# Sliding-window attention rewritten around 32-row scores that are made twice

## The chip, the cores and the metric

The kernel runs on one core of one Trainium2 chip. The metric is the device time of one execution in microseconds; the kernel before takes 2570.04 us (median of three runs, 2560.99 to 2573.86). All inputs and outputs are bf16. "Granted clock" is the share of full TensorE speed that the records of the run show. In the lines of the profiles PE is TensorE, PEld its weight loads, DVE VectorE, ACT ScalarE, POOL GpSimd and SP the queue of transfers. Each trace is of one execution.

## The reference, cut to what matters

```python
g = sigmoid((x * gate_w).sum(-1, keepdims=True))
a = A(x, wqkv, wo)         # 32 heads of 20 columns, causal window of 256 of 2048 rows
b = B(x, mem0, Wq, ...)    # 64 segments in sequence, each hands 8 memory rows on
return g * a + (1 - g) * b

# A, the sliding branch
scores = einsum('bhqd,bhkd->bhqk', q, k) * 20 ** -0.5
mask = (i - j >= 0) & (i - j < 256)
p = softmax(where(mask, scores, -1e9)); o = einsum('bhqk,bhkd->bhqd', p, v) @ wo
```

The kernel computes A first, block by block (16 blocks of 128 rows), then the projections of the memory rows that B needs (called the tail here), then B (the recurrent branch), then the mix. Only A is rewritten. Because of the window, a block of 128 queries meets three blocks of keys.

## The kernel before: what the change touches

Per head, the scores of a block are three 128x128 products. They contract all 128 rows: the queries of one head of four are kept in a tile that is zero in the other 96 rows (`QTm`), the keys of four heads lie together. The masks are added by further products.

```python
def st_scores(h):
    g, r = h // 4, h % 4
    sp = ps_s.tile([P, 512], FP32, name="s_ps", tag="s")
    for ci, c in enumerate(kbs):
        need_mask = (c == qb) or (c == qb - (NKB - 1))
        nc.tensor.matmul(sp[:, ci * P:(ci + 1) * P], lhsT=qm[r][:, g, :], rhs=kring[c][:, g, :],
                         start=True, stop=not need_mask)
        if need_mask:
            nc.tensor.matmul(sp[...], lhsT=ident[:], rhs=(m_last if c == qb else m_first)[:], start=False, stop=True)
    nmx = hp.tile([P, 1], FP32, name="a_nmx")
    nc.vector.tensor_reduce(out=nmx[:], in_=sp[:, 0:nk * P], axis=AX.X, op=ALU.max, negate=True)
    nc.scalar.activation(out=ex[:, 0:nk * P], in_=sp[:, 0:nk * P], func=ACT.Exp, bias=nmx[:], scale=1.0)

def st_transpose(h):      # for two heads: 6 transposes into pt_ps, then one copy to SBUF
    ...
    nc.tensor.transpose(pt_ps[:, a, ci, :], ex[:, ci * P:(ci + 1) * P], ident[:])
    ...
def st_pv(h):             # values: transposed probabilities times V, with a column of ones for the sum
    ...
```

The block ends with the output projection. The B weights that stay in SBUF are loaded in two parts: 34 tiles of 384 KB early, during A, and the rest after A.

```python
early, late, last = weights.resident[:34], weights.resident[34:-3], weights.resident[-3:]
...
branch_A(...)                                   # takes the early ones along
for u in late:
    weights.load_resident(post, u, nc.gpsimd)   # all issued at A's end
tail_projections(tc, weights, xTb, xbqk, xbv)
```

## Time and profile before

| Stage (profiled run, us) | before |
|---|---|
| first maximum | 26.4 |
| sliding branch ends (first tail product) | 526.1 |
| tail projections | 180.9 |
| recurrent branch | 1834.1 |
| mix | 30.0 |
| span | 2571.1 |
| granted clock in the branch, 130 us to 60 us before its end | 0.954 |

The stages are cut at the first product of the next stage in the trace. The page's slices, the table by stretch, the chain and the groups that this rests on are in the prediction. One row of the page is not there and will matter: the granted clock, in tenths, in 40 slices of 64.3 us. The kernel before runs at full speed nearly everywhere:

```profile
PEclk9999999899999999999999999999999999999996
```

### The profile page before, as it was taken

What the parts mean: (1) busy time and instruction counts of PE and PEld (TensorE: products, weight loads), DVE (VectorE), ACT (ScalarE), POOL (GpSimd) and SP (SyncE); (2) the same over time, 40 slices, a digit from 0 to 9 for tenths busy, and PEclk for the clock granted to TensorE, in tenths of its full rate; (3) what the DMA queues carried; (4) which work ended last, traced back from release to release, by engine and by line L of the source; (5) the groups of instructions that cost most, each with busy time, mean ns of one, the idle gap of its engine ahead of it and who ended that gap; (6) DMA issues with size and microseconds to landing.
All of it is one profiled execution on the core that took longest, in us unless ns stands there. A gap on an engine that the chain in (4) does not pass through costs nothing.

```text
span 2571.1 us, 114087 instructions
## 1 busy us (share of the span) xinstructions
PE 2226.3 (87%) x49877; PEld 1645.7 (64%) x49893; DVE 1198.7 (47%) x3578; ACT 1124.3 (44%) x2433; POOL 702.2 (27%) x1973
## 2 busy tenths in 40 slices
PE   7889888889889888888888888888888888889885
PEld 5777777679456665666656666656666566566663
DVE  5777777623234443444444344434443344344434
ACT  4777777622234333433333343333333343333333
POOL 7622222040122222222222222222222222222220
PEclk9999999899999999999999999999999999999996
DMA  6600000075578888888888888888888888888887
GB/s 210 202 17 18 17 17 15 9 252 148 144 242 277 265 263 263 276 266 278 269 259 269 271 275 266 264 256 270 265 266 270 255 268 273 268 266 270 268 258 228
DMA packets 293747, 561.63 MB, mean 218 GB/s; under 512 B 104568, under 2 KB 114048, under 8 KB 293248
## 3 DMA queue, kind: packets, MB, share of 16 engines
q1 hardware_dynamic: 266032, 495.28, 60.5%
q0 software_dynamic: 24256, 55.62, 7.3%
q8 instruction: 391, 6.41, 1.0%
q10 hardware_dynamic: 2960, 3.44, 0.4%
q14 instruction: 108, 0.88, 0.1%
HBM read 524.83 MB, written 36.51 MB: 218 GB/s over the span
## 4 chain that ended last, share of the span: by engine, by line
PE 53%; DMA 33%; ACT 9%; DVE 2%; issue 2%; SPq 0%; ACTq 0%; POOL 0%; DVEq 0%
DMA t_w<-w_packed 30%; PE ps_o L771 8%; PE ps_k L601 7%; PE ps_q L601 7%; PE ps_v L601 6%; ACT a_ex L195 4%; PE t_psum L440 4%; ACT a_pt L208 3%; PE qk_ps L124 3%; PE ps_pv L747 3%; PE tr_k L616 2%; PE t_psv L457 2%; PE S_ps L673 1%; PE pt_ps L205 1%; PE s_ps L187 1%
## 5 line engine op out<-in xcount | busy, mean ns | idle before, releaser
L601 PEld LDWEIGHTS <-t_hT 128*32 128x32 bf16 x15360 | 381.5, 98 | 292.3 <-issue 70.3
L771 PE MATMUL ps_o<-t_OT,t_w 128*128 128x40 bf16 x7040 | 290.5, 180 | 116.0 <-DMA t_w<-w_packed 108.7
L771 PE MATMUL ps_o<-t_OT,w_o 128*128 128x40 bf16 x8320 | 320.8, 180 | 48.0 <-ACT t_OT L752 45.2
L771 PEld LDWEIGHTS <-t_w 128*128 128x128 bf16 x7040 | 226.3, 96 | 136.9 <-DMA t_w<-w_packed 133.5
L771 PEld LDWEIGHTS <-w_o 128*128 128x128 bf16 x8320 | 267.0, 96 | 58.0 <-issue 48.4
L195 ACT ACTIVATE a_ex<-s_ps,a_nmx 128x384 bf16<-128x384 f32 (+2 forms) x512 | 252.8, 576 | 64.4 <-DVE a_nmx L193 64.2
L648 POOL COPY t_K<-t_xqk 128x64 bf16<-128x64 bf16 x256 | 60.9, 238 | 779.6 <-PE S_ps L673 779.6
L193 DVE TENSOR_REDUCE a_nmx<-s_ps 128x1 f32<-128x384 f32 (+2 forms) x512 | 247.0, 523 | 34.7 <-PE s_ps L190 25.4
L601 PE MATMUL ps_v<-w_v,t_hT 128*32 128x384 bf16 x4864 | 254.6, 337 | 0.1
L752 ACT CAST t_OT<-ps_pv 128x480 bf16<-128x480 f32 x256 | 143.2, 559 | 251.6 <-PE ps_pv L747 247.9
L601 PE MATMUL ps_q<-w_q,t_hT 128*32 128x384 bf16 x4096 | 223.0, 340 | 18.7 <-DVE t_hT L782 18.4
L639 DVE COPY t_K<-tr_k 128x256 bf16<-128x256 bf16 x256 | 74.6, 291 | 344.7 <-PE tr_k L616 344.4
L601 PE MATMUL ps_k<-w_k,t_hT 128*32 128x384 bf16 x4096 | 221.8, 339 | 0.0
L606 ACT CAST t_tok<-ps_k 128x384 bf16<-128x384 f32 x256 | 122.7, 479 | 206.3 <-PE ps_k L601 206.3
L625 ACT COPY b_QT<-tr_q 128x384 bf16<-128x384 bf16 x256 | 123.3, 482 | 180.1 <-PE tr_q L616 180.1
L730 DVE TENSOR_TENSOR t_PTx<-PT_ps,mk_x 128x320 bf16<-128x320 f32 x256 | 125.9, 492 | 153.2 <-PE PT_ps L723 153.1
L606 ACT CAST t_tok<-ps_q 128x384 bf16<-128x384 f32 x256 | 122.6, 479 | 145.8 <-PE ps_q L601 145.8
L683 DVE TENSOR_REDUCE sm_mx<-S_ps 128x4 f32<-128x160 f32 x256 | 82.2, 321 | 209.6 <-PE S_ps L673 209.0
L187 PE MATMUL s_ps<-KT_blk,QTm 128*128 128x128 bf16 x1440 | 172.0, 224 | 5.8 <-ACT a_ex L195 5.4
L606 ACT CAST t_vtok<-ps_v 128x384 bf16<-128x384 f32 x256 | 122.7, 479 | 103.7 <-PE ps_v L601 103.7
L561 POOL DMA_DIRECT2D t_xqk<-xbqk x256 | 137.4, 537 | 84.0 <-POOL b_QT L629 39.1
L205 PE MATMUL pt_ps<-a_ident,a_ex 128*128 128x128 bf16 x1440 | 146.4, 221 | 8.3 <-ACT a_ex L195 1.0
(138 smaller groups left out, 4469.2 us busy)
## 6 DMA issues: line engine op xcount, KB each, us to landing
t_w<-w_packed SPq DMA_DIRECT2D x704, 320.0 KB, 4.2
t_w<-w_packed SPq DMA_DIRECT2D x576, 384.0 KB, 4.4
xbqk<-t_qk SPq DMA_DIRECT2D x16, 768.0 KB, 4.3
t_xqk<-xbqk POOLq DMA_DIRECT2D x256, 48.0 KB, 3.7
w_v<-in_B_Wv_dram POOLq DMA_DIRECT2D x19, 384.0 KB, 8.2
w_q<-in_B_Wq_dram POOLq DMA_DIRECT2D x16, 384.0 KB, 5.2
w_k<-in_B_Wk_dram POOLq DMA_DIRECT2D x16, 384.0 KB, 6.9
xbv<-t_vt SPq DMA_DIRECT2D x64, 96.0 KB, 1.8
```

Source lines behind the costliest of these rows:

```text
L187: nc.tensor.matmul(sp[:, ci * P:(ci + 1) * P], lhsT=qm[r][:, g, :], rhs=kring[c][:, g, :], start=True, stop=not need_mask)
L193: nc.vector.tensor_reduce(out=nmx[:], in_=sp[:, 0:nk * P], axis=AX.X, op=ALU.max, negate=True)
L195: nc.scalar.activation(out=ex[:, 0:nk * P], in_=sp[:, 0:nk * P], func=ACT.Exp, bias=nmx[:], scale=1.0)
L205: nc.tensor.transpose(pt_ps[:, a, ci, :], ex[:, ci * P:(ci + 1) * P], ident[:])
L440: nc.tensor.matmul(pt[:, bb, :], lhsT=ws[ki][kt][:, c:c + P], rhs=xTb[:, kt, t * P:(t + 1) * P], start=(kt == 0), stop=(kt == KT - 1))
L561: sc.op("DMA", 500, lambda: nc.gpsimd.dma_start(tile_of(qk)[:].rearrange("p i b t -> p (i b t)"), xbqk[s, :, g].rearrange("p i c -> p (i c ...
L601: nc.tensor.matmul(t[32 * j:32 * j + 32, 0:384], lhsT=tile_of(hT)[:, kt, :], rhs=w[:, j * 384:(j + 1) * 384], start=(kt == kts[0]), stop=( ...
L606: sc.op("ACT", act(384), lambda: nc.scalar.copy(tile_of(tok)[:], b["tile"][:, 0:384]), reads=[b], writes=[tok])
L625: nc.scalar.copy(dst, tq["tile"][:].rearrange("p b (j t) -> p b j t", t=SEG))
L730: nc.vector.tensor_tensor(out=tile_of(dst)[:], in0=PT["tile"][:, i, :, :].unsqueeze(2).to_broadcast([P, 2, 4, L]), in1=mk.unsqueeze(1).uns ...
L752: sc.op("ACT", act(480), lambda: nc.scalar.copy(tile_of(OT)[:].rearrange("p b j l -> p (b j l)"), o["tile"][:, 0:480]), reads=[o], writes= ...
L771: nc.tensor.matmul(t[:, dt * L:(dt + 1) * L], lhsT=w[:, r * D + dt * P:r * D + (dt + 1) * P], rhs=OT["tile"][:, b, i, :], start=(g == 0 an ...
```

## The change

The transposes of the probabilities, their copies and the mask products are to go. Scores are made twice. The first time (32 rows contracted, in one of four row groups, the 32-row strips of the array: 20 rows of the head, 12 spare) only their masked maximum is taken, in one VectorE operation. The maxima are put into two of the spare rows of the queries (in one negated and rounded to bf16, in the other what the rounding left), and the keys carry 1 and -1 there. The second time the product is made the other way round, keys by queries, so that it comes out transposed and with its maximum already subtracted; ScalarE takes the exponential straight into the tile that the value products read, and GpSimd zeroes what the mask forbids. Counted from the newest block of queries that a product needs, the second scores lag the first by 22 heads and the values by 32; projections of the next block and the output projection are spread over the heads. To make room in SBUF, 14 more weight tiles move from early to late.

```diff
+    # scores: maxima only
+    nc.tensor.matmul(sp[:, i * P:(i + 1) * P], lhsT=rows(qt_[t], h), rhs=rows(kt_[c], h), start=True, stop=True,
+                     tile_position=(32 * (h % 4), 0))
+    nc.vector.tensor_tensor_reduce(out=junk[:, 0:n], in0=sp[:, 0:n], in1=mask[:, NKB * P - n:], op0=ALU.add, op1=ALU.max,
+                                   scale=1.0, scalar=-3.0e38, accum_out=mx[t, h // HH][:, h % HH:h % HH + 1])
...
+    # augment: add the negated maxima to the spare rows of the queries
+    nc.tensor.matmul(ap[:]..., lhsT=ident[:], rhs=qt_[t][half][:]..., start=True, stop=False, skip_group_check=True)
+    for g in range(4):
+        nc.tensor.matmul(ap[:, g, :], lhsT=mt[:, g]..., rhs=ident[:], start=False, stop=(g == 3), skip_group_check=True)
...
+    # probs: transposed scores, exponential, selection
+    nc.tensor.matmul(tp[:, i * P:(i + 1) * P], lhsT=rows(kt_[c], h), rhs=rows(qa_[q], h), start=True, stop=True,
+                     tile_position=(32 * (h % 4), 0))
+    nc.scalar.activation(out=pt[:, r, 0:n], in_=tp[:, 0:n], func=ACT.Exp)
+    nc.gpsimd.affine_select(out=pt[:, :, 0:P], in_=pt[:, :, 0:P], compare_op=ALU.is_ge, fill=0.0, base=0,
+                            pattern=[[0, 4], [1, P]], channel_multiplier=-1)
...
+    # every step: the products of the two kinds are issued in turn
+    for i in range(3):
+        for a in mms:
+            if i < len(a):
+                a[i]()
...
-    early, late, last = weights.resident[:34], weights.resident[34:-3], weights.resident[-3:]
+    early, late, last = weights.resident[:20], weights.resident[20:-3], weights.resident[-3:]
```

(Cut: pools, evacuations, the augmentation's small operations, the queue of projections. `rows(t, h)` is the 32-row strip of head h. The list of resident weights is also put in the order in which the tail uses them: queries and keys by group, then values and outputs.)

## The prediction

> **What bounds the kernel now.** I read the stage table first (busy time per engine in each stretch), then the groups of the sliding branch, then its chain of waits and a few microseconds of the timeline. The page's slices separate three stages, and the change touches the first:
>
> ```profile
> PE   7889888889889888888888888888888888889885
> ACT  4777777622234333433333343333333343333333
> POOL 7622222040122222222222222222222222222220
> DMA  6600000075578888888888888888888888888887
> ```
>
> One slice is 64.3 us. ScalarE at seven tenths marks the sliding branch (slices 1 to 8). In the timeline its last output projection starts at 523.08 and the first tail projection at 526.09, so the branch costs 526 us. The tail projections last to about 700 and the recurrent branch to the end; about 2045 us are not rewritten. Two blocks of 128 rows in the middle of the branch:
>
> ```profile
> 200.00:231.00 31.00, 27.66 (x459) 23.61 (x459) 23.48 (x53) 24.08 (x46) 6.78 (x15) 0.94 0.05 15
> 231.00:262.00 31.00, 28.60 (x465) 24.70 (x463) 24.41 (x53) 23.73 (x46) 5.90 (x11) 0.93 0.04 11
> ```
>
> Columns: length, then busy time and count of TensorE, its weight loads, VectorE, ScalarE, GpSimd, then granted clock, DMA share, GB/s. TensorE is busy 90%, the two vector engines 77%: no single wait carries the block, TensorE leads and is stalled by the others. The chain shows where:
>
> ```profile
> 157.73 1.91 ACT a_ex L195 x4
> 160.49 2.37 ACT a_ex L195 x5
> 166.46 1.04 PE out_ps L255 x4
> 188.85 1.91 ACT a_ex L195 x4
> 191.61 2.37 ACT a_ex L195 x5
> 197.57 2.30 PE out_ps L255 x9
> ```
>
> Start, duration, what. Each block ends in a serial tail (last exponentials, transposes, values, output projection), and one block is 197.57 - 166.46 = 31.1 us. Later ones are up to 33 (230.03 to 262.94). Some tails run at half clock: in the last block the loads before the 512-column products are 0.425 us apart, while an earlier tail had four products in 1.04 us.
>
> TensorE's own work in a block: 160 score and mask products, 96 transposes of probabilities, 80 Q/K products and 10 other transposes, 346 at 0.055 us (18 Q products took 1.16 us, one alone 0.22: 0.94/17) = 19.0; 96 value products at 0.027 (six took 0.31, one 0.174) = 2.6; V and output projection 2.7; gate 0.1. Sum 24.5 us. So 6.5 us of a 31.1 us block are stalls and lost clock.
>
> [...]No instruction of this trace uses row groups; its column groups do overlap: sixteen 384-column products of the recurrent branch took 0.83 us[...].
> [...]three transposes of 0.056 us start at 1311.60 and the next product, in another mode, at 1311.88, so 0.11 us are lost; the change at 1311.33 lost 0.09. I use 0.1.
> [...]the 128x384 exponential with its maximum as bias takes 576, the 128x384 cast 479.
> [...]the 128x320 product took 480 to 492 ns[...].
>
> The rows for the operations replaced:
>
> ```profile
> L195 ACT ACTIVATE a_ex<-s_ps,a_nmx 128x384 bf16<-128x384 f32 x201 | 103.4, 596 | 28.2 <-DVE a_nmx L193 28.1
> L193 DVE TENSOR_REDUCE a_nmx<-s_ps 128x1 f32<-128x384 f32 x203 | 103.3, 548 | 12.5 <-PE s_ps L190 10.6
> L205 PE MATMUL pt_ps<-a_ident,a_ex 128*128 128x128 bf16 x600 | 57.9, 220 | 2.9
> L208 ACT COPY a_pt<-pt_ps 128x768 bf16<-128x768 bf16 x50 | 40.6, 811 | 11.4 <-PE pt_ps L205 11.1
> L131 POOL COPY QTm<-QT_blk 20x512 bf16<-20x512 bf16 x50 | 30.3, 606 | 43.5 <-ACT QT_blk L129 41.4
> L210 DVE COPY a_pt<-pt_ps 128x768 bf16<-128x768 bf16 x49 | 27.1, 553 | 10.1 <-PE pt_ps L205 9.4
> ```
>
> After the bar: busy us, mean ns, idle before with its main releaser.
>
> **The change part by part, for one full block.**
> TensorE: 64 mask products and 96 transposes go; 96 transposed scores come, and two augmentations of one 512-column and four 128-column products (2 x (0.216 + 0.22) = 0.9 us). Both score kinds contract 32 rows. The lag of 22 heads puts them in row groups two apart, and they are issued alternately into different PSUM banks, so I count each pair as one: 96 x 0.056 = 5.4. With 90 Q/K and transpose products 5.0, values 2.6, V and output 2.7, gate 0.1 and augmentation 0.9, the sum is 16.7. Against it, nearly every head now has 128-row work between the 32-row products: 28 of 32 heads x 2 changes x 0.1 = 5.6. Total 22.3, or 23.2 at a granted clock of 0.96.
> VectorE: 32 fused mask-and-maximum operations replace 32 reductions. [...]the 8 copies of probabilities go. 17.9 + 4.2 for K evacuation (2 x 0.69), x transpose 0.48, normalization (2 x 0.75) and small ones = 22.1.
> ScalarE: 32 exponentials at 0.48 instead of 0.59, 8 copies of 0.81 gone, 2 evacuations of 0.6 and one gate product added: 15.4 + 4.7 = 20.1, down from 24.
> GpSimd: 16 causal selections of 128x512. The 128x128 one at the start took 0.29, a memset of that size 0.205 and one of 5120 columns 4.36 (0.85 ns a column, fixed about 0.1), so 512 columns are about 0.1 + 4 x 0.19 = 0.87; 13.9 us, plus some 6 of copies, small operations and DMA issue, minus the 8 head copies. It has room, with ten heads of slack before its result is read.
>
> So TensorE 23.2 and VectorE 22.1 stand nearly level. The serial tail of the block disappears, since projections queue among the heads; I leave 3 us for stalls of two level engines with two score buffers each: 26 us, 0.82 us per head step.
>
> The whole branch is 512 score steps plus 96 steps of drain. Start: the five weight pieces are all requested at once (now the third waits until 12.5 us), and the first maximum moves from 26.4 to about 17 us. Steps 0 to 85 have no probabilities: 17 (128 columns) + 19 (256) + 16 (22 steps) = 52. Steps 86 to 511: 426 x 0.82 = 349. Drain, no VectorE maxima: 96 x about 0.42, limited by the exponential and two buffers, plus 4 for the last projection = 44. Sum 462 against 526: 64 us less, hence 2506.
> Fourteen more weight tiles of 384 KB (5.4 MB, about 21 us of transfer at the 252 GB/s of that stage) load after the branch. The tail projections need the first of them only after two of four groups, some 53 us later; DMA is 54 to 79% busy there. I count zero.
>
> **Rivals.**
> (a) Row groups do not overlap, or the scheduler breaks the alternation (it already runs two blocks' ten x transposes together at 10.72). Then 96 x 0.056 = 5.4 us come back, TensorE is 28.8 at that clock and the block 30 to 31: 426 x 0.95 = 405, the branch 518, the kernel about 2562. The overlapping column groups speak against it.
> (b) VectorE or GpSimd becomes the bound. A fused maximum with 0.1 us more for writing its result gives 25.3 on VectorE, block about 28.5, 2535. GpSimd in order, with late selections, would hold back values to a similar time. For it: VectorE's margin is only a microsecond; against: GpSimd had 78% idle.
> (c) The stall allowance is too large, as every producer now leads its reader by many heads. At 0.74 a step 34 us more go: about 2472. A V buffer that comes free later than the program asks for it (five buffers, read up to five blocks later) could instead push V work back into bursts.
> (d) The later weights starve the tail projections: at most the 21 us, against it the 53 us of lead.
>
> **Range and chances.** The sum says 2506; (c) seems as likely as (b), and lost half-clock tails return a little, so I put 2502. Two per cent is 2518.6, that is 51 us saved; a step of 0.85 reaches it. (a) alone lands within 2%. Slower than 2621 would need the branch to grow by 51 us. So 0.66 faster, 0.30 the same, 0.04 slower; 2455 to 2553.
>
> **What would show it.** Right: branch end near 460 us; score and transposed-score products starting pairwise within a few ns; exponentials near 0.48; the fused maximum near 0.56; a steady block of 26 us with TensorE and VectorE both over 80% busy, granted clock near 1; tail and recurrent stages unchanged. Wrong: single products 55 ns apart in the score steps, the maximum over 0.65, GpSimd over 90% busy, or tail projections waiting for w_q or w_k.

## The result, and the profile after

The changed kernel is correct and slower: 2663.04 us median (2656.42 to 2698.24, four runs, one of them, 2698, slow) against 2567.22 (2560.99 to 2573.86, four runs). The ratio of the fast runs is 1.0364, 95% interval 1.0316 to 1.0413. Here and below a ratio is the mean time of one kernel's fast runs over the mean of the other's fast runs of the same rounds, so it is not quite the ratio of the medians quoted beside it.

| Stage (profiled runs, us) | before | after | difference |
|---|---|---|---|
| first maximum | 26.4 | 19.1 | |
| sliding branch ends | 526.1 | 589.0 | +63 |
| tail | 180.9 | 193.8 | +13 |
| recurrent branch | 1834.1 | 1842.5 | +8 |
| mix | 30.0 | 30.3 | 0 |
| span | 2571.1 | 2655.7 | +85 |
| granted clock in the branch, as above | 0.954 | 0.604 | |

In the other profiled runs below the unchanged recurrent branch took 1828 to 1843 us, so its +8 is scatter. The branch and the tail have to be explained. The page of the changed kernel, the rows that answer to those of before:

```profile
PE   8999999987988888888889888888889888888885
ACT  1555455551223333333334334333334333333333
POOL 5733333334022222222222222222222222222220
PEclk7757556658999999999999999999989999999997
DMA  6300000019557888888888888888878888888887
```

TensorE is busier in the branch than before (slices 2 to 8), ScalarE has gone from seven tenths to five, as was meant, and the granted clock stands at five to seven tenths instead of nine. The same stretches of 33 us in both kernels, first before, then after (columns as in the prediction):

```profile
200.00:233.00 33.00, 29.66 (x472) 25.06 (x472) 24.49 (x55) 24.08 (x46) 6.78 (x15) 0.91 0.06 17
300.00:333.00 33.00, 29.30 (x480) 24.81 (x479) 24.73 (x56) 24.66 (x48) 6.95 (x15) 0.95 0.06 17
```

```profile
200.00:233.00 33.00, 32.14 (x413) 20.25 (x411) 20.02 (x73) 18.79 (x42) 12.44 (x29) 0.70 0.06 17
300.00:333.00 33.00, 32.19 (x375) 19.82 (x373) 18.38 (x67) 16.97 (x38) 12.70 (x28) 0.55 0.04 12
```

TensorE does fewer products in the stretch (375 to 413 instead of 472 to 480; a full block has 413 now by the program and had 467) and is busy 97% of it. No other engine is over 61%. So the branch is bound by TensorE alone, at 0.55 to 0.70 of its speed. The chain of waits shows the pace of the blocks by the output projection:

```profile
287.08 2.15 PE out_ps L256 x5
324.69 2.15 PE out_ps L256 x5
362.38 2.15 PE out_ps L256 x5
400.19 2.15 PE out_ps L256 x5
```

A block takes 37.6 to 37.8 us, where 26 were predicted. Five products of 512 columns in 2.15 us are 0.43 each, the half-clock pace that the prediction had met in before's block tails (0.425). Not every block is like this: of the ten blocks between 119 and 473 us (from the starts of the transposes of x) seven take 37 to 39 us and three 29 to 30.

The groups of the operations that the change put in, between 200 and 400 us:

```profile
L173 DVE CUSTOM_DVE_ANT_0 a_junk<-s_ps,a_mask 128x384 bf16<-128x384 f32 x180 | 96.0, 556 | 83.9 <-PE st_ps L203 52.8 <-PE s_ps L166 29.4
L211 ACT ACTIVATE a_pt<-st_ps 128x384 bf16<-128x384 f32 x180 | 82.4, 492 | 53.9 <-PE st_ps L203 48.8 <-PE s_ps L166 4.2
L166 PE MATMUL s_ps<-KT,QT 32*128 32x128 bf16 x537 | 72.8, 280 | 0.3
L203 PE MATMUL st_ps<-QA,KT 32*128 32x128 bf16 x537 | 71.1, 282 | 2.0 <-ACT a_pt L211 1.9
L216 POOL TENSOR_SCALAR_AFFINE_SELECT a_pt<-a_pt 128x512 bf16<-128x512 bf16 x45 | 28.5, 634 | 0.0
```

VectorE and ScalarE work at the predicted durations (0.556 and 0.492 us) and wait for TensorE (83.9 and 53.9 us idle). Did the row groups overlap, the question of rival (a)? The timeline of one step:

```profile
301.93 0.28 PE L166 MATMUL s_ps<-KT,QT 32*128 32x128 bf16 x1
301.93 0.28 PE L203 MATMUL st_ps<-QA,KT 32*128 32x128 bf16 x1
...
302.00 0.31 PE L166 MATMUL s_ps<-KT,QT 32*128 32x128 bf16 x1
...
302.01 0.31 PE L203 MATMUL st_ps<-QA,KT 32*128 32x128 bf16 x1
...
302.11 0.31 PE L166 MATMUL s_ps<-KT,QT 32*128 32x128 bf16 x1
302.12 0.31 PE L203 MATMUL st_ps<-QA,KT 32*128 32x128 bf16 x1
302.35 0.34 PEld L131 LDWEIGHTS <-WkP 128*128 128x128 bf16 x4 [0.20 <-issue]
302.36 0.50 PE L131 MATMUL qk_ps<-xT_blk,WkP 128*128 128x128 bf16 x3
```

They did: score and transposed score start 0.00 to 0.01 us apart, and pairs are about 0.1 us apart, what 128 columns take at half clock (0.107, a quarter of 0.43). After the last pair 0.24 us pass until a full-array product starts, 0.135 more than 0.107. Between 130 and 460 us the median over 84 such steps at half clock, from a 32-row product to a full-array one of 128 columns, is 0.241. I count this loss as the cost of the mode change, from products on a row group to products on the full array or back.

The clock records of the branch show only full and half speed (1.0 and 0.5), in pieces of 3.41 us and multiples. Between 130 and 460 us the changed kernel spends 261 of 330 us at half. There it starts 2,697 products in 261 us, at full speed 1,114 in 69 us. For a block of 413 this makes 40.0 us at half and 25.6 us at full: at full speed the block would have been what was predicted. The question for the chip is what took the clock away from an array that is busy 97% of the time.

**A law for the clock, from the traces.** I cut the traces into the 3.413 us windows of the clock records and counted in each the columns that the products stream, weighting a product by its contracted rows over 128 (a 32-row product counts a quarter). In these traces a window is at full speed if the window before it had more than about 2,990 such columns, with the misses given below. At full speed some 8,100 columns of full-array products fit (512 columns take 0.216 us in e9; the 169 products of 512 columns that e6 starts in 36 us make up to 8,200 a window; the expectations below take 8,192, and a half or a quarter of it). The cut was fitted on before and after, where it misses 3 of 149 and 6 of 168 windows up to the end of the branch, so there it is a description. It stands in the expectation of e1, before any experiment was built; on the ten traces of the experiments it misses 43 of 1,594 windows. Other counts do worse on all twelve traces (1,911 windows), each with its own best cut: weighted columns miss 49, columns not weighted by rows 324, the number of products 440. And windows that follow a fast one and windows that follow a slow one, fitted apart, have nearly the same cut (2,970 and 3,050): in these traces it is an amount of work per time, whatever the speed at which it was done. The sections of e6 and e9 test the law directly.

The law has two stable states. A block of the changed kernel has 28,100 weighted columns: 80 x 128 for Q and K, 10 x 128 for transposes, 6,400 for V and output, 96 x 21 for values, 2,048 for augmentation, and the 192 scores only 192 x 128 / 4 = 6,144. At full speed that is 28,100 x 3.413 / 25.6 = 3,750 a window, above the cut; at half speed 28,100 x 3.413 / 40.0 = 2,400, below. By the law one thin window throws TensorE into half speed, and an average one does not bring it back. The kernel before has some 53,000 in 31 us, 5,800 a window.

### The profile page after: what moved, and what is told of

Read it like the earlier page. It is cut to its first block, busy times and chain, and to the rows that moved or that the text cites. A ratio compares the mean times of both kernels' runs of the same rounds, so it can differ in the third digit from the quotient of the medians.

```text
span 2655.7 us, 112871 instructions
## 1 busy us (share of the span) xinstructions
PE 2336.8 (88%) x49093; PEld 1617.9 (61%) x49093; DVE 1142.3 (43%) x3894; ACT 1051.0 (40%) x2369; POOL 791.6 (30%) x2187
## 4 chain that ended last, share of the span: by engine, by line
PE 60%; DMA 33%; ACT 3%; issue 2%; DVE 1%; POOL 0%; SPq 0%; another core or an unknown queue 0%; ACTq 0%; DVEq 0%; POOLq 0%
DMA t_w<-w_packed 30%; PE ps_k L658 8%; PE ps_q L658 7%; PE ps_o L828 7%; PE ps_v L658 6%; PE qk_ps L131 5%; PE s_ps L166 4%; PE t_psum L497 4%; PE st_ps L203 3%; PE ps_pv L804 2%; PE tr_k L673 2%; PE o_ps L230 2%; PE S_ps L730 1%; PE out_ps L256 1%; PE v_ps L148 1%
## 5 line engine op out<-in xcount | busy, mean ns | idle before, releaser
L173 DVE CUSTOM_DVE_ANT_0 a_junk<-s_ps,a_mask 128x384 bf16<-128x384 f32 (+2 forms) x512 | 261.4, 531 | 198.3 <-PE st_ps L203 97.6
L211 ACT ACTIVATE a_pt<-st_ps 128x384 bf16<-128x384 f32 (+2 forms) x512 | 224.8, 471 | 122.9 <-PE st_ps L203 104.1
L203 PE MATMUL st_ps<-QA,KT 32*128 32x128 bf16 x1440 | 196.1, 274 | 12.4 <-ACT a_pt L211 10.5
L166 PE MATMUL s_ps<-KT,QT 32*128 32x128 bf16 x1440 | 196.4, 270 | 2.1 <-DVE a_mx L173 1.2
```

The source lines that it names most:

```text
L166: nc.tensor.matmul(sp[:, i * P:(i + 1) * P], lhsT=rows(qt_[t], h), rhs=rows(kt_[c], h), start=True, stop=True, tile_position=(32 * (h % 4) ...
L173: nc.vector.tensor_tensor_reduce(out=junk[:, 0:n], in0=sp[:, 0:n], in1=mask[:, NKB * P - n:], op0=ALU.add, op1=ALU.max, scale=1.0, scalar= ...
L203: nc.tensor.matmul(tp[:, i * P:(i + 1) * P], lhsT=rows(kt_[c], h), rhs=rows(qa_[q], h), start=True, stop=True, tile_position=(32 * (h % 4) ...
L211: nc.scalar.activation(out=pt[:, r, 0:n], in_=tp[:, 0:n], func=ACT.Exp)
```

## The experiments

All outputs are right. The times of before in the three groups of runs were 2568.12 (2557.16 to 2585.97; e1 to e4), 2569.23 (2561.15 to 2580.98; e5 to e8) and 2562.65 (2551.49 to 2572.05; e9, e10). A table first; clock and branch are those of the stage table above. A change counts as faster or slower from 2%.

| Run | us, median (range) | ratio to before [95%] | branch ends | tail | clock |
|---|---|---|---|---|---|
| e1 full-array extras | 2643.54 (2633.77 to 2651.18) | 1.0283 [1.0240, 1.0325] | 580.9 | 195.0 | 0.845 |
| e2 32-row extras | 2666.74 (2650.39 to 2690.86) | 1.0365 [1.0313, 1.0417] | 598.3 | 195.0 | 0.738 |
| e3 128-row scores | 2536.33 (2534.00 to 2545.84) | 0.9885 [0.9850, 0.9920] | 474.9 | 200.3 | 0.991 |
| e4 before, late weights | 2574.60 (2562.50 to 2587.36) | 1.0028 [0.9979, 1.0076] | 525.7 | 192.9 | 0.954 |
| e5 e3 and mode changes | 2586.89 (2574.81 to 2595.96) | 1.0067 [1.0019, 1.0116] | 520.0 | 198.8 | 0.990 |
| e7 e3, weights paced | 2538.51 (2531.55 to 2547.48) | 0.9884 [0.9842, 0.9926] | 474.9 | 195.3 | 0.994 |
| e8 after, weights paced | 2651.98 (2636.55 to 2668.08) | 1.0321 [1.0251, 1.0390] | 603.8 | 181.9 | 0.599 |
| e10 e3, weights paced finer | 2526.41 (2514.54 to 2540.62) | 0.9861 [0.9819, 0.9903] | 477.6 | 185.6 | 0.987 |

The theory is that the clock follows the array work in a window. The rivals: TensorE is slow because of the work itself (too many products and mode changes), or the mode changes, which cost 0.135 us each at half clock, lower the clock.

### e1: useless full-array products added

```diff
+            for _ in range(2):   # once a score step, results never read
+                nc.tensor.matmul(sp[:, NKB * P:512], lhsT=ident[:], rhs=ident[:], start=True, stop=True)
```

> The changed kernel plus two full-array products of 128 columns in every score step (256 columns, 8192 a block), written beside the scores and never read. Theory (the granted clock of each window of 3.41 us follows the array work of the window before: columns times rows/128, threshold about 2990): a block's work rises from 28.1 to 36.3 thousand column-equivalents, at full clock some 4400 a window, so the clock in the branch rises from about 0.6 to 0.75-0.95 and, though work was added, the branch ends earlier: 490 to 560 us instead of 589, the kernel 2560 to 2630. Rival (TensorE is simply overloaded, by mode changes and small products; the clock has another cause): [...]branch end near 695, kernel near 2765.

The clock rose from 0.604 to 0.845 in the range expected, and the kernel got faster with 64 products more a block (fast runs 2633.77 to 2651.18, after 2656.42 to 2668.71; the intervals of the two ratios just overlap). But the branch ended at 581, outside the 490 to 560 that I gave, and the kernel above 2560 to 2630; 581 is no clear gain on 589, given the scatter of 15 us that e8 will show. (The rival's 695 is 589 and some 110 us, what 512 x 256 columns take at 0.43 us for 512.) The same stretches as above:

```profile
200.00:233.00 33.00, 32.69 (x454) 20.69 (x453) 19.48 (x71) 19.09 (x41) 12.13 (x28) 0.84 0.06 17
300.00:333.00 33.00, 32.69 (x451) 20.67 (x450) 19.76 (x71) 18.71 (x41) 12.29 (x28) 0.84 0.06 17
```

TensorE starts more products than in after (451 to 454) and is still full. The extras stand apart from other full-array work, so a block has 42 mode changes each way instead of 31, and between 130 and 460 us it is still at half speed for 91 of 330 us. The clock's direction fits the theory; the added work ate most of the gain.

### e2: the same extras with 32 rows

```diff
+                nc.tensor.matmul(sp[:, NKB * P:512], lhsT=rows(qt_[t], h), rhs=rows(kt_[t], h), start=True, stop=True,
+                                 tile_position=(32 * (h % 4), 0))
```

> The control of the run before: the same 256 added columns a step, but as 32-row products in the row group of the scores. Theory: they count a quarter, a block's work is 30.1 thousand, at half clock (37.7 + 6.8 us a block) 2310 a window, under the threshold: clock stays at 0.5-0.65, branch end 640 to 700, kernel 2710 to 2770. If only TensorE's busy time or the number of products mattered to the clock, this run would gain as the one before: branch end 490 to 560.

This is the control for e1, and it missed on all three counts: clock 0.738 (I had 0.5 to 0.65), branch 598, kernel 2667. The order is right (32-row extras raise the clock less than full-array ones and do not make the kernel faster), the size is not. The trace shows what the forecast left out. Its slow windows have 2,400 weighted columns on average and its fast ones 3,500 (130 to 460 us), so like the changed kernel it can stay in either state, and its blocks take about 31 or about 41 us. Which state holds is decided by single windows near the cut, and a block's average, from which I forecast, does not tell it. The law fits worst here, with 12 of 170 windows missed. What tipped more windows upward than in the changed kernel was not separated and stays open.

### e3: the same algorithm with 128 rows contracted

The keys of each head of four are copied into tiles that are zero in the other 96 rows (by GpSimd, which had room), so that both score kinds contract 128 rows. No product is saved or added, pairs no longer overlap, and there are no mode changes. It needs SBUF, so only 8 weights are loaded early.

```diff
+        ktm = [[[const.tile([P, 4, P], BF, ...) for r in range(4)] for i in range(2)] for b in range(5)]   # zeroed once
...
+                        for r in range(4):
+                            nc.gpsimd.tensor_copy(ktm[t % 5][half][r][32 * r:32 * r + 32], kt_[t][half][32 * r:32 * r + 32])
...
-    nc.tensor.matmul(sp[...], lhsT=rows(qt_[t], h), rhs=rows(kt_[c], h), ..., tile_position=(32 * (h % 4), 0))
+    nc.tensor.matmul(sp[...], lhsT=allr(qt_[t], h), rhs=krow(c, h), start=True, stop=True)
-    nc.tensor.matmul(tp[...], lhsT=rows(kt_[c], h), rhs=rows(qa_[q], h), ..., tile_position=(32 * (h % 4), 0))
+    nc.tensor.matmul(tp[...], lhsT=krow(c, h), rhs=allr(qa_[q], h), start=True, stop=True)
-    early = weights.resident[:20]
+    early = weights.resident[:8]
```

> Scores and transposed scores contract 128 rows: K is kept in four copies per half with the other heads' rows zero (8 GpSimd copies a block). No mode changes, no overlapped pairs, the same results. 12 weight tiles fewer load early, to make room. Theory: work per block 46.5 thousand, clock above 0.92 through the branch, TensorE about 22 us and VectorE 22 to 24 us a block, block 26 to 28 us, branch end 460 to 495; the tail stage is some 10 to 30 us longer for the later weights; kernel 2520 to 2570. Rival (clock has another cause, e.g. projections spread out): clock about 0.6, branch end over 560, kernel over 2630.

```profile
200.00:233.00 33.00, 31.80 (x523) 27.89 (x522) 24.07 (x91) 24.39 (x55) 23.49 (x47) 1.00 0.06 17
300.00:333.00 33.00, 31.40 (x530) 27.50 (x529) 24.13 (x89) 22.45 (x51) 21.81 (x47) 1.00 0.11 33
```

Everything came as expected but VectorE, which is busy 19.7 us a block and not 22 to 24. TensorE is as busy as in the changed kernel but starts 523 to 530 products in the time of 375 to 413, because the clock is 1.00. A block takes 26 us, the branch ends at 475, and the kernel is 1.2% faster than before (the interval lies below 1) although TensorE gives up the overlap of row groups. This is the undoing of one part of the change, and it accounts for the loss in the branch: the rest of the change is a gain.

### e5: mode changes put into e3

e3 took away two things, thin work and mode changes. Here one 32-row product of a single column per score step brings the mode changes back without array work.

```diff
+                nc.tensor.matmul(sp[:, NKB * P:NKB * P + 1], lhsT=rows(qt_[t], h), rhs=rows(kt_[t], h)[:, 0:1],
+                                 start=True, stop=True, tile_position=(32 * (h % 4), 0))
```

> This is the version with 128-row scores (e3) with one 32-row product of a single column added to every score step: two mode changes more per step, next to no array work. Theory (the granted clock follows the array work, columns times rows, in a window of 3.41 us): the work stays near 46,500 columns a block, so the clock in the branch stays at 0.95 or above; the drains alone cost 64 x 0.095 us = 6 us a block, with the added products 6 to 8 us, so a block goes from 25.8 to 32 to 34 us, the branch ends at 550 to 585 us, the kernel takes 2590 to 2650 us. Rival (the mode changes themselves[...] lower the clock): clock 0.75 or less in the branch, the branch ends after 620 us, the kernel takes over 2680 us.

```profile
200.00:233.00 33.00, 32.93 (x519) 27.42 (x517) 23.83 (x86) 21.53 (x48) 21.16 (x43) 1.00 0.06 17
```

The clock stays at 0.990, so the rival that mode changes lower it falls. They cost time only: a block goes from about 26.3 to 28.9 us (mean of block starts), 2.6 us where I expected 6 to 8. The branch ends at 520, earlier than my 550 to 585, and the kernel at 2586.89 us, just below my 2590 to 2650. The starts of neighbouring products show why. Each step loses 0.20 us by the two changes (0.105 from the one-column product to the next full one, 0.098 the other way), some 6 us a block as predicted. But in e3 the products of a block, counted from start to start beyond the time that their own columns take, already waited 4.4 us; in e5 only 0.6 us of waiting is left beside the changes. So most of what the changes cost (the drains of the expectation) lies in time that was idle anyway.

### e6 and e9: sections of pure products

The kernel before with TensorE work in front of it that has no other engine in it. The moving operands are zeros (in e9 the weights are an identity).

```diff
+    # e6: n products of 512 columns; groups 0: 128 rows; 1, 2, 4: 32 rows on so many row groups in turn
+    SECTIONS = [(180, 0), (240, 2), (80, 1), (140, 2), (240, 4), (140, 0)]
```

> The kernel before with a row of pure TensorE sections in front, all back to back, 512 columns a product: 180 full-array products, 240 of 32 rows on two row groups in turn, 80 of 32 rows on one row group, 140 on two groups again, 240 on four groups, 140 full-array. Theory (a window stays or becomes fast only if columns x rows / 128 in it pass some 2,990 of the possible 8,192): after warming, full speed in the first section; full speed in the second (two groups at once give 4,096 a window); half speed in the third after one window (2,048); still half speed in the fourth, the same work as the second but entered slow (2,048 a window at half speed); full speed again within two windows in the fifth (four groups at half speed give 4,096); full speed in the last. Rival 1 (what counts is the time in which TensorE is busy at all): full speed in all six. Rival 2 (32-row products count as full ones or not at all): second and fourth alike. Kernel time 2710 to 2770 us, which tells nothing.

The sections in order, each without the time of change between two (columns as before; the last but two is the clock):

```profile
5.00:41.00 36.00, 36.00 (x169) 16.28 (x168) 4.46 (x8) 0.00 (x0) 28.00 (x51) 1.00 0.74 228
42.00:67.00 25.00, 25.00 (x235) 11.22 (x236) 0.00 (x0) 0.00 (x0) 8.20 (x17) 1.00 0.23 63
73.00:99.00 26.00, 26.00 (x62) 8.95 (x61) 0.00 (x0) 0.00 (x0) 0.00 (x0) 0.50 0.00 1
100.00:128.00 28.00, 28.00 (x134) 9.56 (x131) 0.00 (x0) 0.00 (x0) 0.00 (x0) 0.50 0.00 1
133.00:143.00 10.00, 10.00 (x189) 4.64 (x185) 0.00 (x0) 0.00 (x0) 0.00 (x0) 1.00 0.01 3
144.00:173.00 29.00, 29.00 (x137) 13.11 (x135) 0.00 (x0) 0.00 (x0) 0.00 (x0) 1.00 0.00 1
```

TensorE is busy 100% in every row. All six came as the theory said. One row group alone (third row) falls to 0.50 without ever being idle. The second and fourth rows are the same program, two row groups in turn: at 1.00 when entered fast, at 0.50 for 28 us when entered slow. Four row groups entered slow come back to 1.00. So "busy at all" is not what counts (rival 1), and a fixed weight with no memory cannot give two answers for one program (rival 2). In weighted columns a window the second section has some 4,100 (235 products in 25 us), the third 1,040 (62 in 26), the fourth 2,090 (134 in 28) and the fifth, once fast, about 8,200 (189 in 10). The pace agrees with the records: the third section took 400 ns a product on average (its first window still fast), the second 108 (two at once), the last 216. The operands are zeros; the branches above, with real data, have the same cut.

```diff
+    # e9: "h": 64 rows; "c": 128 rows, weights of 32 columns; "t": 128x128 transposes
+    SECTIONS = [(180, 0), (150, "h"), (60, 0), (120, "c"), (60, 0), (640, "t"), (60, 0)]
```

> The kernel before with TensorE sections in front, each entered at full speed: 150 products of 64 rows on one half of the array (512 columns each), 120 products of 128 rows whose weights have only 32 columns, 640 transposes of 128 x 128 in bf16, with runs of full-array products between. If work is columns times rows over 128 and the threshold about 2,990: the 64-row section holds full speed (4,096 a window), the 32-weight-column section holds it too (8,192), the transposes hold it (some 7,500). If the area of the array in use is what counts, the 32-weight-column section falls to half speed (2,048). If transposes do not count, their section falls to half speed. Kernel time 2700 to 2780 us, which tells nothing.

```profile
42.00:74.00 32.00, 32.00 (x149) 13.91 (x148) 0.00 (x0) 0.00 (x0) 7.09 (x15) 1.00 0.15 42
87.00:113.00 26.00, 26.00 (x122) 11.56 (x120) 0.00 (x0) 0.00 (x0) 0.00 (x0) 1.00 0.00 1
127.00:162.00 35.00, 35.00 (x631) 35.00 (x629) 0.00 (x0) 0.00 (x0) 0.00 (x0) 1.00 0.01 2
```

All three hold full speed: half the rows (which needs the cut to be below some 4,050), a quarter of the weight columns (so it is rows that count, not the area of the array), and transposes (640 of them, which the trace lists as MATMUL). The sections were entered fast, so they show what holds full speed, not what brings it back.

### e4 and e8: the late weights alone, and paced

e4 is the kernel before with only the weights part of the change (20 early instead of 34, in the new order).

```diff
-    early, late, last = weights.resident[:34], weights.resident[34:-3], weights.resident[-3:]
+    early, late, last = weights.resident[:20], weights.resident[20:-3], weights.resident[-3:]
```

> The kernel before with only the change's weight part: 20 weight tiles early instead of 34, in the new order. Theory: sliding branch unchanged (526 us), the first tail store of q and k lands later behind 41 weight loads instead of 27, the tail stage is 181 + 13 us; kernel 2578 to 2590. Rival (the 13 us of the changed kernel came from elsewhere): 2565 to 2575.

Its tail is 192.9 us, 12 longer than before's and the same as in the changed kernel; in the whole time (ratio 1.0028, interval across 1) this cannot be seen. The 2574.60 us even lie in the range that I gave the rival, so it is the tail that speaks against it: with 27 late loads it takes 180 to 183 us in three traces (before, e6, e9), with 41 it takes 193 to 195 in four (after, e1, e2, e4). The chain of the changed kernel and its table by stretch show the way it happens:

```profile
597.74 32.58 DMA xbqk<-t_qk
```

```profile
604.00:614.00 10.00, 8.73 (x157) 8.61 (x155) 0.00 (x0) 0.42 (x1) 5.14 (x10) 1.00 1.03 413
614.00:624.00 10.00, 0.00 (x0) 0.00 (x0) 0.00 (x0) 0.00 (x0) 5.27 (x10) 0.57 1.03 415
624.00:634.00 10.00, 2.81 (x27) 2.81 (x27) 2.30 (x4) 2.00 (x4) 6.31 (x14) 0.50 0.98 325
```

The first store of projected queries and keys is issued at 597.74 and holds up the chain for 32.58 us, since 41 weight loads were issued at once and fill the DMA engines (DMA share 1.03, 413 GB/s). There are two staging tiles; both wait for their stores, the evacuations for the tiles, and TensorE has no product at all from 614 to 624. So it is the store, not a missing weight, that waits. e8 releases three loads per stored block, each tied to that block's result:

```diff
+                for u in [later.pop(0) for _ in range(min(3, len(later)))]:
+                    weights.load_resident(post, u, nc.gpsimd, st[:, 0, 0, 0, 0:1])   # writes one column first
...
-        for u in late:
-            weights.load_resident(post, u, nc.gpsimd)
```

> The changed kernel with its 41 later weights released three at a time in the tail. Theory: the tail shrinks from 194 to 180 to 186 us, the branch stays at 580 to 600 us with a clock near 0.6, the kernel takes 2640 to 2660 us. Rival: the tail stays at 190 us or more and the kernel at 2655 to 2675 us.

```profile
604.00:614.00 10.00, 10.00 (x177) 10.00 (x176) 2.77 (x4) 2.34 (x4) 6.27 (x17) 0.97 0.84 267
614.00:624.00 10.00, 10.00 (x183) 10.00 (x180) 3.36 (x5) 2.34 (x4) 5.65 (x11) 1.00 1.11 317
624.00:634.00 10.00, 10.00 (x184) 10.00 (x180) 2.68 (x5) 2.86 (x5) 7.04 (x20) 1.00 1.10 319
```

This stall is gone and the tail is back at 181.9. (The kernel before has a small one of the same kind: from 546 to 556 us its TensorE is busy 3.09 of 10. Pacing its loads was not tried.) The branch of this run ended at 603.8, above the 580 to 600 that I gave, at a clock of 0.599; its code is the same as in the changed kernel, so some 15 us of a branch end at half clock can be scatter between runs.

### e7 and e10: the better version, with paced weights

Both are e3 with the loads of e8. e3 has 53 late tiles; e7 issues 12 at once and four per stored block, e10 five and three.

```diff
-        for u in late:
+        for u in late[:12]:    # e10: 5
...
+                for u in [later.pop(0) for _ in range(min(4, len(later)))]:   # e10: 3
```

> The version with 128-row scores (e3), with the later weights loaded a few at a time: after each block of stored queries and keys four loads are released (the first of each writes a column of its tile from that block's result), instead of all at once at the branch's end. Theory (the tail is long because its first stores queue behind the burst of weight loads): the tail shrinks from 200 to 181 to 188 us, the kernel takes 2510 to 2530 us, ratio 0.978 to 0.985. Rival (the tail is long for another reason, the clock or the order of its products): the tail stays at 195 to 203 us, the kernel within 6 us of e3's 2536.

> e7 with fewer loads at once: 5 of the later weights at the end of the branch (12 in e7), then three per block of stored queries and keys (four in e7). Theory: e7's TensorE stood still at 495 to 505 us because its 12 loads at once held up the first store; with 5 the tail goes from 195 to 182 to 190 us, the kernel takes 2518 to 2532 us, ratio 0.980 to 0.986. Rival: 53 loads are too many for the first half of the tail however they are ordered, the tail stays at 192 us or more and the ratio at 0.987 to 0.990.

e7 was a miss, in the range that I gave the rival: the tail shrank only from 200.3 to 195.3 and the time not at all. Its table by stretch still shows a hole (TensorE busy 3.19 of 10 us at 495 to 505 us), and its waits show the same cause: from 475 to 560 us the evacuations waited 40.0 and 35.0 us for stores of queries and keys.

```profile
495.00:505.00 10.00, 3.19 (x58) 3.07 (x56) 0.26 (x1) 0.29 (x1) 1.07 (x3) 0.86 1.06 367
```

e10 brings the tail to 185.6, inside the 182 to 190 expected, with the kernel at 2526.41 us; its ratio of 0.9861 just misses the 0.980 to 0.986 that I gave. Its interval overlaps e3's 0.9885, so only the tail in the trace is shown to be shorter than e3's, not the whole time. Both are faster than the kernel before, with intervals below 1 though under 2%, and than the changed one.

## Why the prediction was wrong, point by point

- **The step that failed is "Total 22.3, or 23.2 at a granted clock of 0.96".** The prediction carried the clock of the kernel before over to a loop with other work. It had expected "granted clock near 1" and measured 0.604. The weighted work of a block fell from some 53,000 columns to 28,100, and that is too little to hold full speed. The clock records of the branch know two speeds, in windows of 3.41 us, and show half speed for 261 of 330 us. I had taken an array that is not idle for one at full speed, and e6 shows an array that is never idle at half speed (0.50 for 26 us). What I missed could have been found blind only in part: before's trace has 16 windows at half speed between 40 us and the end of its branch (the prediction even quotes one of its block tails), and 15 of them follow windows with fewer than 2,990 columns; but before has no 32-row product in its branch from which to learn their weight.
- **What this cost.** Predicted branch 462, measured 589, so 127 us. e3 has the same steps at full clock and ends at 475, its first maximum 6 us later than in the changed kernel (24.9 against 19.1, since it zeroes more tiles). An estimate from these for the changed kernel at full clock is 469. The clock then accounts for about 120 of the 127 us, and the sum of the prediction was some 7 us short; with e8's scatter of 15 us neither is exact.
- **The mechanisms of TensorE were right.** That products on different row groups run at once was my estimate: before's trace shows it only of column groups (sixteen 384-column products in 0.83 us, where 384-column products on the full array start 0.162 us apart). Here pairs start within 0.01 us, so rival (a) fell. 31 mode changes each way in a block (predicted 28) lose about 0.095 us at full and 0.135 us at half clock (predicted 0.1). A block at full speed would take 25.6 us by the estimate above (predicted 26).
- **VectorE, ScalarE and GpSimd were right.** The fused maximum took 0.556 (0.56 predicted, an estimate; before's trace gives the same, the 0.492 of its 128x320 product and 64 more columns at the pace of its reductions, 0.281, 0.412 and 0.548 us for 128, 256 and 384 columns), the exponential 0.492 (0.48), the selection 0.634 (0.87 estimated, too much). Rival (b) feared 0.1 us for writing the maximum. The write is there, a second instruction of 0.083 us, but it starts before the first is shown to end, and back to back the pairs come 0.48 us apart. VectorE is busy 20.2 us a block (22.1 predicted), and rival (b) fell: neither engine is over 61% busy. One reading was off: the exponential of before takes 592 ns at the median, only the shortest take the 576 that the prediction names, so its maximum as bias costs about 0.1 us by after's 492.
- **The later weights: "I count zero" was wrong.** They cost 12 to 13 us (e4, e8). The prediction asked whether the weights come in time, and they do; it did not ask what else uses the DMA queues. Rival (d), "at most the 21 us", was right in size; its way was another, a store that waits behind the loads.
- **No rival named the clock.** The four rivals gave 2472 to 2562 and "at most the 21 us". A chance of 0.04 for slower was the consequence: all rivals were about waits and counts, none about the speed of the engine that carries everything.

## What to carry to other kernels

Work that leaves TensorE only a part of its rows was paid twice here: it also took away the work that held the clock. Before a product is narrowed, add up columns times rows over 128 for the 3.4 us windows of the loop and compare with what the trace needs for full speed (here about 2,990); near that line, contracting zeros over the full array was faster than overlapping narrow products (475 us against 589). And when loads are moved to a later stage, ask which stores there will queue behind them, not only when the loads are needed.
